# Decays of the first batch as TensorE products in the score banks of a fused attention and MoE kernel

## The chip, the cores and the metric

The kernel runs on one core of one Trainium2 chip. The metric is the device time of one launch in microseconds (us), the median of several runs; for the kernel before it is 889.91 us over three runs (888.77 to 890.62). Differences below about 0.2% (1.8 us) cannot be told from no change. The names of the engines are those of the profile: PE is TensorE (PEld its weight loads), ACT is ScalarE, DVE is VectorE, POOL is GpSimd, SP is SyncE, which issues the DMAs.

## The reference

Eight batches of eight heads, 576 positions, head size 64. Each head's scores get a decay (the difference of two cumulative sums of log f) and a causal mask, then a softmax; the attention output, 4608 rows of 512, goes through three matrices whose products are maximised and a fourth one.

```
scores = scale * np.matmul(q, k.transpose(0, 1, 3, 2))          # B, H, S, S = 8, 8, 576, 576
cum    = np.cumsum(np.log(np.clip(f, 0.0001, 1.0)), axis=-1)
decay  = cum[:, :, :, None] - cum[:, :, None, :]
scores = np.where(causal, -1e9, scores + decay)
attn   = np.exp(scores - scores.max(-1, keepdims=True))
attn   = attn / (attn.sum(-1, keepdims=True) + 1e-9)
x      = (attn @ v) laid out as (4608, 512)
h      = max(x @ w1, x @ w2, x @ w3)                              # 512 -> 768
out    = h @ w_out                                               # 768 -> 512
```

A query's own cumulative sum is the same for all its keys and falls out of the softmax; only the key's, with a minus sign, has to be added to the scores.

## The kernel before

Scores are held with keys on partitions and queries on columns. Two methods are in use.

**First batch (8 heads, as 4 pairs).** q and k are loaded in natural order (`load_raw`) and turned by TensorE (`turn_pair`, L568), since this is ready soonest. `scores_pair` (its products are L867) computes a pair of heads at a time: head 0 of the pair uses the array's rows 0 to 63, head 1 rows 64 to 127, each with its own PSUM bank. The 576 queries are cut into four tiles (`TILES`): tile 0 has 256 queries, tiles 1 and 2 have 128, tile 3 has 64; a tile covers 2, 3, 4 and 5 key blocks of up to 128 keys, 14 blocks a pair and head, 1600 columns. For each tile and head:

- pass a (L867): q and k products in fp32 for each block, then the mask as a product of an identity with a mask tile (L874);
- the maximum over a query's keys: ACT copies the first block out of PSUM with the key's decay as its bias (L895); DVE takes the other blocks one by one, adding their decay and taking the maximum in one instruction (L901); POOL's `partition_all_reduce` then takes the maximum over the partitions (L904);
- pass b (L886): TensorE subtracts that maximum from the bank (a product with a matrix that holds -1 in row 0 of each half);
- the exponential, once for each block, again with the block's decay as bias (L911).

The decays for the biases come from the cumulative sum (`decay`): five transposes on TensorE (L530) and two copies by DVE put the negated sums of the first eight heads into `CT`, keys on partitions. For the later batches the negated sums, split into a high and a low part, go to DRAM (`cdram`) and come back as two extra rows of k. `values_first` (L931 products with v, L941 sums), `finish_first` (row sums to DRAM and back, the division) and `split_first` (high and low part of x) follow.

**Later batches (56 heads).** `scores` (products L747, maxima L806 and L813, POOL L816, exponentials L830) takes a head at a time from loaded and transposed data; here decays are already in the products.

**The MoE part** (`moe`, `gemm1` L1092, `gemm2` L1123) runs in fp32r with high and low parts, three products for one. Its weights (12 loads of 1 MB) arrive as raw words, are converted on ACT and DVE (`convert`, L584, L587, L589) and split (`split`, L594, L595). All of TensorE's gemm work of a batch is interleaved with the scores of the next.

**What sets the order.** The kernel does not issue instructions in the order in which it is written. Every step is handed to a planner (`Plan.add`) with an engine, a cost, what it reads and writes, and a due time (`prio`); `Plan.emit` runs a list schedule over these costs and issues the steps in the order that comes out, a fixed order for each engine. `MOVES` is a table of 41 shifts of due times, most of them drawn from a seed. `GATES` names the steps after which the first six weight loads may be issued. `Slot` objects let a step take any free PSUM bank; `retire` orders the reuse of buffers under another name. Within an engine instructions start in that order only, so one that waits holds up all behind it.

```
add("ACT", act_cost(blocks[0][2]), lambda j=j, m=m: nc.scalar.activation(
    m, bank(j)[:, 0:nq], AF.Identity, bias=bias(0, j)), [kb[j], "ct"], [ks[j]], prio)
...
add("ACT", act_cost(w), lambda j=j, c=c, w=w, col=col, to=to, p=p: nc.scalar.activation(
    p[0:nk(c), to:to + w], bank(j)[0:nk(c), col:col + w], AF.Exp, bias=bias(c, j)), [kb[j], "ct", "ct4"],
    [f"e{pi % 2}/{t}{j}{c}"], prio, drop=(slots[j],))
```

Of the kernel before, what the change touches and what calls it, by code (L numbers as in the profile page):

```python
# [277 lines left out]
def kernel(  # L278
# [69 lines left out]
    LX = sb("pl2", [P, P + S1])  # L348
    LESS = LX[:, 0:P].bitcast(F32R)
    HLT = sb("hl", [P, 2, 2, 2, S], F32R)  # L350
    HL = {"k": HLT[:, 0], "q": HLT[:, 1]}
    CSX = sb("pl1", [P, 2 * S])
    CS = CSX[0:BH].bitcast(F32R).rearrange("p (t s) -> p t s", t=2)
# [10 lines left out]
    CT = sb("ct", [P, 5 * H])  # L364
# [149 lines left out]
    def decay():  # L514
# [1003 lines left out]
```

## Time and profile before

| | |
|---|---|
| median of three runs | 889.91 us (888.77 to 890.62) |
| profiled execution, device time | 891.11 us |
| its span, first to last instruction | 889.3 us |
| outside the span | 1.81 us |
| PE busy in the span | 865.4 us (97%) |
| DVE, ACT, POOL busy | 651.5, 406.4, 360.1 us |
| mean granted TensorE clock | 0.987 of 2.4 GHz |
| weights and other DMA traffic | 111.48 MB |

Busy time counts a stretch once, however many instructions of the engine overlap in it; a group's busy time in a list by lines adds the instructions up. A busy PE is not a PE at its peak: at the lower granted clock it does half the work in the same time. The granted clock has two levels, 1.2 and 2.4 GHz, so that a mean of 0.89 over a stretch says that 22% of it ran at 1.2 GHz. The wait of an instruction is put down to the engine whose work ended last before it started.

### The profile page before, as it was taken

Reading aid. Unit: us, or ns where it says so; the run is one execution under the profiler, and the core shown is the slowest. Engines: PE = TensorE matmul, PEld = TensorE weight load, DVE = VectorE, ACT = ScalarE, POOL = GpSimd, SP = SyncE. Lnnn points to the kernel's source line nnn. Section 1 sums busy time; section 2 is a strip of 40 time slices with the busy share of each in tenths; the row PEclk is TensorE's granted clock in tenths of the full one; section 3 lists DMA queues with packets and bytes.
Section 4 is the critical chain, followed back from the end, with each engine's and each line's share of the span. In section 5 each row is a group of like instructions: output and inputs, shape, how many; then the busy total and the mean of one; then the engine's idle time right before and its main releaser. Section 6 shows DMA issues by size and latency. Waiting matters only on the chain.

```text
span 889.3 us, 17657 instructions
## 1 busy us (share of the span) xinstructions
PE 865.4 (97%) x6437; PEld 772.7 (87%) x6437; DVE 651.5 (73%) x1405; ACT 406.4 (46%) x1014; POOL 360.1 (40%) x200
## 2 busy tenths in 40 slices
PE   8977899999999999999999999999999999999998
PEld 5655788898988999998988989898998989899997
DVE  3566896758767786678777786578867697788990
ACT  4787663545434443445334453344434443344431
POOL 2342322144455355544554355535544544540000
PEclk9888899999999999999999999999999999999999
DMA  7637867654555454564455355455545464300001
GB/s 168 200 99 196 268 165 178 162 134 138 114 149 143 102 144 102 146 145 122 120 142 141 92 152 126 134 120 158 120 103 155 104 169 97 92 11 15 24 1 60
DMA packets 99518, 111.48 MB, mean 125 GB/s; under 512 B 61432, under 2 KB 62200, under 8 KB 99432
## 3 DMA queue, kind: packets, MB, share of 16 engines
q1 hardware_dynamic: 99432, 110.35, 47.2%
q8 instruction: 51, 0.84, 0.4%
q14 instruction: 35, 0.29, 0.1%
HBM read 50.74 MB, written 9.88 MB: 68 GB/s over the span
## 4 chain that ended last, share of the span: by engine, by line
PE 93%; ACT 4%; DMA 1%; SPq 1%; DVE 1%; POOL 1%; issue 0%; ACTq 0%; DVEq 0%; POOLq 0%
PE s L1092 25%; PE mp L1092 15%; PE s L1123 10%; PE mp L1123 6%; PE t L1092 6%; PE s L747 5%; PE mp L747 4%; PE mp L1005 4%; PE s L1005 3%; PE s L1288 3%; PE mp L1288 2%; PE t L1005 2%; PE t L747 1%; PE t L1288 1%; ACT w L911 1%; PE s L931 1%
## 5 line engine op out<-in xcount | busy, mean ns | idle before, releaser
L845 POOL PARTITION_ALL_REDUCE z<-va_s x48 | 174.5, 3635 | 272.7 <-DVE va_s L840 134.2
L1092 PE MATMUL s<-xh_r,w_r 128*128 128x256 f32 (+1 forms) x1096 | 259.5, 297 | 0.0
L1092 PEld LDWEIGHTS s<-xh_r,w_r 128*128 128x128 f32 x1096 | 189.1, 188 | 4.0 <-issue 2.2
L1092 PE MATMUL mp<-xh_r,w_r 128*128 128x256 f32 (+1 forms) x672 | 165.5, 296 | 0.0
L816 POOL PARTITION_ALL_REDUCE gm<-mx x56 | 118.0, 2108 | 114.7 <-DVE mx L806 92.5
L1092 PE MATMUL s<-xl_r,w_r 128*128 128x256 f32 (+1 forms) x548 | 161.8, 295 | 0.0
L1092 PEld LDWEIGHTS mp<-xh_r,w_r 128*128 128x128 f32 x672 | 118.4, 188 | 2.8 <-issue 2.2
L1092 PEld LDWEIGHTS s<-xl_r,w_r 128*128 128x128 f32 x548 | 103.0, 188 | 0.9
L1092 PE MATMUL mp<-xl_r,w_r 128*128 128x256 f32 (+1 forms) x336 | 99.1, 295 | 0.0
L647 DVE STREAM_TRANSPOSE hl<-hl 128x576 f32<-128x576 f32 x56 | 66.2, 1240 | 16.7 <-DMA hl<-in_k_dram 7.3
L747 PE MATMUL s<-qs_r,ks_r 128*128 128x320 f32 (+4 forms) x334 | 71.9, 297 | 1.8 <-POOL qs_r L818 1.8
L1123 PE MATMUL s<-w_r,hmh_r 128*128 128x512 f32 x216 | 68.8, 400 | 0.0
L1092 PE MATMUL t<-xh_r,w_r 128*128 128x320 f32 (+1 forms) x248 | 67.7, 305 | 0.0
L747 PE MATMUL mp<-qs_r,ks_r 128*128 128x320 f32 (+4 forms) x256 | 60.3, 298 | 4.0 <-DMA ks_r<-hl 4.0
L1092 PEld LDWEIGHTS mp<-xl_r,w_r 128*128 128x128 f32 x336 | 63.1, 188 | 0.3
L1106 ACT ACTIVATE hmh_r<-tm 128x256 fp32r<-128x256 f32 x84 | 34.9, 416 | 60.7 <-DVE tm L1103 60.2
L1108 DVE TENSOR_TENSOR hml_r<-tm,hmh_r 128x256 fp32r<-128x256 f32 x84 | 53.5, 638 | 7.7 <-ACT hmh_r L1106 7.3
L747 PEld LDWEIGHTS s<-qs_r,ks_r 128*128 128x128 f32 (+1 forms) x334 | 53.3, 182 | 5.7 <-POOL qs_r L818 2.5
L1103 DVE TENSOR_TENSOR tm<-s,tm 128x256 f32<-128x256 f32 (+1 forms) x88 | 39.4, 449 | 21.2 <-ACT tm L1101 9.6
L806 DVE TENSOR_TENSOR mx<-mx,s 128x320 f32<-128x320 f32 (+3 forms) x112 | 47.3, 422 | 6.6 <-ACT mx L813 3.2
L747 PEld LDWEIGHTS mp<-qs_r,ks_r 128*128 128x128 f32 (+1 forms) x256 | 42.2, 181 | 7.3 <-DMA ks_r<-hl 4.4
L1092 PEld LDWEIGHTS t<-xh_r,w_r 128*128 128x128 f32 x248 | 46.2, 192 | 1.3 <-issue 1.0
(461 smaller groups left out, 1978.1 us busy)
## 6 DMA issues: line engine op xcount, KB each, us to landing
qs_r<-hl SPq DMA_DIRECT2D x168, 144.0 KB
ks_r<-hl SPq DMA_DIRECT2D x168, 144.0 KB
w<-in_moe_w_dram SPq DMA_DIRECT2D x9, 1024.0 KB
out_dram<-o_r SPq DMA_DIRECT2D x35, 256.0 KB
hl<-in_k_dram SPq DMA_DIRECT2D x14, 576.0 KB
hl<-in_q_dram SPq DMA_DIRECT2D x14, 576.0 KB
r_r<-rdram SPq DMA_DIRECT2D x56, 144.0 KB
vn<-in_v_dram SPq DMA_DIRECT2D x30, 128.0 KB
```

Source lines behind the costliest of these rows:

```text
L647: add("DVE", 1085, lambda e=e, tt=tt, xs=xs: nc.vector.transpose(tt[:, e], xs[:, e]), [key + "0"], [key + "1"], prio)
L747: nc.tensor.matmul(bank[bk][0:l.shape[-1], col:col + w], l, rhs(qa, w), start=start and bk not in begun, stop=stop, skip_group_check=True)
L806: nc.vector.tensor_tensor(mt[:, a:a + w], mt[:, a:a + w], bank[bk][:, col:col + w], op=ALU.max)
L816: add("POOL", 450 + 2.6 * nq, lambda: nc.gpsimd.partition_all_reduce(gm, mt, P, bass.bass_isa.ReduceOp.max), [km, km + "a"], [kg], prio - ...
L845: add("POOL", 520 + 5.1 * nq, lambda: nc.gpsimd.partition_all_reduce(Z[:, 0:S], blocks_sum()[:, 0:S], P, bass.bass_isa.ReduceOp.add), ["s1 ...
L1005: nc.tensor.matmul(t[D * j:D * j + D, qa:qa + w], vn[:, j, c, 0:D], prs[u][j][0]()[:, col:col + w], start=y == 0, stop=True, skip_group_ch ...
L1092: nc.tensor.matmul(m(), unit_w(i, fb)[:, w, kt, :], xx, start=kt == 0 and x == 0, stop=kt == KT - 1 and x == 2,)
L1103: add("DVE", dve_cost(cn), lambda m=m: nc.vector.tensor_tensor(t, m(), t, op=ALU.max), [km, kt_], [kt_], prio + EV, drop=(slot,))
L1106: add("ACT", act_cost(w) + 40, lambda hh=hh, a=a, d=d, w=w: nc.scalar.activation(hh()[:, fb, d:d + w], t[:, a:a + w], AF.Copy), [kt_], [kh ...
L1108: add("DVE", dve_cost(w), lambda hh=hh, hl=hl, a=a, d=d, w=w: nc.vector.tensor_tensor(hl()[:, fb, d:d + w], t[:, a:a + w], hh()[:, fb, d:d ...
L1123: nc.tensor.matmul(BANKS[slot.bank][:, 0:cn], l[:, fb, cs], unit_o(fb)[:, r, ds], start=fb == 0 and x == 0, stop=fb == FT - 1 and x == 2,)
L1288: nc.tensor.matmul(bank[c](), w(tw)[:, k], mat(x)[:, tx, k], start=new and k == 0 and z == 0, stop=k == 1 and z == 2, skip_group_check=True)
```

## The change

For the first batch the key's decay no longer comes in as a bias of ACT and DVE instructions, but is added to the score bank by TensorE.

- `decay()` no longer turns the sums for `CT`. DVE writes their negated high part to partitions 0 to 31 of a tile `BT` and the low part to 32 to 63; ACT copies both to partitions 64 to 127. `SEL` is a selection matrix with a one where a partition's head is the wanted one, made from the identity.
- `scores_pair` gets a step `decays()` between pass a and the maxima: one fp32r product for each block and head, whose stationary operand is the block's part of `BT` (64 rows) and whose moving operand is one column of `SEL`, broadcast over the block's queries. That makes 28 products a pair, 112 in all.
- Maxima: one `tensor_reduce` over all of a tile's blocks for each head, read from PSUM, 32 in all in place of 80 instructions of DVE. Only tile 0, whose blocks have different widths, keeps a copy on ACT (of 128 columns, 8 in place of 32).
- Exponentials: no bias, so one instruction takes several blocks: 384 columns in tiles 0, 1 and 2, a further 128 in tile 2, and 192 and 128 in tile 3. 48 in all in place of 112.
- The sums for the later batches (`CS`) lie in `MX` and `GM` and go to DRAM in two DMAs; row sums and reciprocals of the first batch lie elsewhere; mask products of tile 3 have 128 output rows.
- The planner's table `MOVES` has 783 entries in place of 41, and due times (`A2`, `B1`, `WP`), `GATES`, and some planner costs differ. This moves instructions in the whole program.

```
-    CT = sb("ct", [P, 5 * H])
+    CS = MX[0:BH].bitcast(F32R), GM[0:BH]
...
+    CSX = sb("pl1", [P, 2 * S], F32R)
+    BT, LESS, SEL = CSX[:, 0:S], CSX[:, S + 256:S + 384], CSX[:, S + 384:S + 384 + H]
...
-        add("PE", 400, turn, ["pf1", "idf"], ["sp2"], DP, rows=H)
-        add("DVE", 130, lambda: nc.vector.tensor_scalar(CT[:, 0:4 * H], SP2[:, 0:4 * H], -1.0, None, op0=ALU.mult), ["sp2"], ["ct"], DP)
-        add("DVE", 110, lambda: nc.vector.tensor_scalar(CT[0:64, 4 * H:], SP2[0:64, 4 * H:5 * H], -1.0, None, op0=ALU.mult), ["sp2"], ["ct4"], DP)
...
+        x = PF[1][0:32, 0:S]
+        add("DVE", 369, lambda: nc.vector.tensor_scalar(BT[0:32], x, -1.0, None, op0=ALU.mult), ["pf1"], ["bt0"], DP, port=1.0)
+        add("ACT", act_cost(S), lambda: nc.scalar.activation(BT[64:96], BT[0:32].bitcast(F32), AF.Copy), ["bt0"], ["bt2"], DP)
+        add("DVE", 669, lambda: nc.vector.scalar_tensor_tensor(
+            BT[32:64], x, -1.0, BT[0:32].bitcast(F32), op0=ALU.mult, op1=ALU.subtract), ["pf1", "bt0"], ["bt1"], DP, port=1.0)
+        add("ACT", act_cost(S), lambda: nc.scalar.activation(BT[96:128], BT[32:64].bitcast(F32), AF.Copy), ["bt1"], ["bt3"], DP)
...
+        def decays():
+            for c, qa, w, col in blocks:
+                for j in range(2):
+                    one = SEL[half(j), 2 * pi + j:2 * pi + j + 1].broadcast_to((D, w))
+                    nc.tensor.matmul(bank(j)[0:nk(c), col:col + w], BT[half(j), keys(c)], one, start=False, stop=False,
+                                     skip_group_check=True)
...
         for j in range(2):
             m = mt[:, nq * j:nq * j + nq]
-            add("ACT", act_cost(blocks[0][2]), lambda j=j, m=m: nc.scalar.activation(
-                m, bank(j)[:, 0:nq], AF.Identity, bias=bias(0, j)), [kb[j], "ct"], [ks[j]], prio)
-
-            def most(j=j, m=m):
-                for c, qa, w, col in blocks[1:]:
-                    x = m[0:nk(c), qa - q0:qa - q0 + w]
-                    nc.vector.scalar_tensor_tensor(x, bank(j)[0:nk(c), col:col + w], bias(c, j), x, op0=ALU.add, op1=ALU.max)
...
+            if t == 0:
+                add("ACT", act_cost(P), lambda j=j, m=m: nc.scalar.activation(m[:, 0:P], bank(j)[:, 0:P], AF.Copy),
+                    [kb[j]], [ks[j] + "a"], prio - CB)
+                m, src, c = m[:, P:], lambda j=j: bank(j)[:, P:384], 2
+            else:
+                src, c = lambda j=j: bank(j)[:, 0:n], len(blocks)
+            add("DVE", 1.05 * n + 150, lambda j=j, m=m, src=src, c=c: nc.vector.tensor_reduce(
+                m, src().rearrange("p (c q) -> p q c", c=c), axis=AX.X, op=ALU.max), [kb[j]], [ks[j]], prio - CB)
...
+                runs = [(0, 3 * nq, lambda p=p: p[1][:, 0:3 * S1].rearrange("p (c y) -> p c y", y=S1)[:, :, q0 - S2:q0 - S2 + nq], x)]
+                if t > 1:
+                    runs.append((3 * nq, n, lambda p=p: p[1][:, 960 + P * (t == 3):960 + P * (t == 3) + n - 3 * nq], lambda v: v))
+            for y, (a, e, dst, view) in enumerate(runs):
+                add("ACT", act_cost(e - a), lambda j=j, a=a, e=e, dst=dst, view=view: nc.scalar.activation(
+                    dst(), view(bank(j)[:, a:e]), AF.Exp), [kb[j]], [f"e{pi % 2}/{t}{j}{y}"], prio, drop=(slots[j],))
...
-        (11.3, 13.3, 0, 21, 0.03), (-20, 100, 1, 61, -0.8), (1.4, 5.4, 0, 4533, 1), (25.8, 26.3, 0, 29917, 0.06),
+        (2.1, 10.1, 0, 43247, 1), (33.3, 34.3, 0, 27900, 0.12), (-20, 100, 1, 22, -0.8), (-5.9, 2.1, 0, 23458, 0.5),
...
-    LEAD, MLAG, WP, WR = 2.1, 2.0, 2.7, 0.65
+    LEAD, MLAG, WP, WR = 2.1, 2.0, 1.0, 0.65
-    A2, A1, B1, UB, TO, XO1 = 0.8, 1.6, 0.4, 0.1, (1, 3, 2), 0.6
-    GATES = ("vn1/0", "vn3/0", "e1/200", "vd0/1", "vd1/1", "vd2/1")
+    A2, A1, B1, UB, TO, XO1 = 0.3, 1.6, 1.5, 0.1, (1, 3, 2), 0.6
+    GATES = ('vn1/0', 'vn3/0', 'e1/000', 'e1/100', 'vd1/2', 'vd1/1')
```

Three places show what moves. On PE, tile 0 of the first pair; L874 are the masks of the kernel before, followed there by warm-up products (L547):

```order
L874 LDWEIGHTS ident
L874 MATMUL s_110<-mask,ident 128x128
L874 LDWEIGHTS ident
L874 MATMUL mp_115<-mask,ident 128x128
L874 LDWEIGHTS ident
L874 MATMUL s_110<-mask,ident 128x128
L874 LDWEIGHTS ident
L874 MATMUL mp_115<-mask,ident 128x128
L547 LDWEIGHTS ident
L547 MATMUL s_108<-ident 128x512
```

The same tile in the changed kernel; L1085 are the masks, L1091 the decays (`pl_70` is the tile that holds `BT` and `SEL`):

```order
L1085 LDWEIGHTS ident
L1085 MATMUL mp_113<-mask,ident 128x128
L1085 LDWEIGHTS ident
L1085 MATMUL t<-mask,ident 128x128
L1085 LDWEIGHTS ident
L1085 MATMUL mp_113<-mask,ident 128x128
L1085 LDWEIGHTS ident
L1085 MATMUL t<-mask,ident 128x128
L1091 MATMUL mp_113<-pl_70 128x256
L1091 MATMUL t<-pl_70 128x256
L1091 MATMUL mp_113<-pl_70 128x128
L1091 MATMUL t<-pl_70 128x128
```

Four products of 64 array rows now stand behind the four masks of 128 rows, two for each head.

On ACT, the exponentials of tile 3 of the first pair before the change (`pf` and `ph` are the two heads):

```order
L911 ACTIVATE pf_76<-t,ct 128x64
L911 ACTIVATE ph_78<-s_109,ct 128x64
L911 ACTIVATE pf_76<-t,ct 128x64
L911 ACTIVATE ph_78<-s_109,ct 128x64
L911 ACTIVATE ph_78<-s_109,ct 64x64
L911 ACTIVATE pf_76<-t,ct 128x64
L911 ACTIVATE pf_76<-t,ct 64x64
L911 ACTIVATE ph_78<-s_109,ct 128x64 x2
L911 ACTIVATE pf_76<-t,ct 128x64
```

And the same tile after it (L1135; L793 before and the tile-0 exponential behind are its neighbours):

```order
L793 ACTIVATE ks_68<-mp_114 128x96x3
L1135 ACTIVATE pf_76<-s_109 128x3x64
L1135 ACTIVATE pf_76<-s_109 128x128
L1135 ACTIVATE ph_78<-s_110 128x128
L1135 ACTIVATE ph_78<-s_110 128x3x64
L1135 ACTIVATE pf_77<-mp_112 128x384
```

Ten instructions have become four, and `ct` is no longer read.

On PE again, the last rows ahead of the first gemm product (L1092) in the kernel before; L747 are scores of the second batch:

```order
L747 MATMUL t<-qs_r,ks_r 128x192
L747 MATMUL s_109<-qs_r,ks_r 64x64
L747 MATMUL mp_114<-qs_r,ks_r 128x448
L747 MATMUL s_110<-qs_r,ks_r 128x256
L747 MATMUL s_111<-qs_r,ks_r 128x448
L747 MATMUL s_108<-qs_r,ks_r 128x256
L760 LDWEIGHTS ident
L760 MATMUL s_111<-mask,ident 128x128
L760 LDWEIGHTS ident
L760 MATMUL s_108<-mask,ident 128x128
L1092 MATMUL t<-xh_r,w_r 128x256
```

In the changed kernel the first gemm product (L1315) stands right behind the row sums of the fourth pair (L1164):

```order
L1164 MATMUL s_108<-w_97,rx_r 32x160 x2
L1164 MATMUL s_108<-w_98,rx_r 32x160 x2
L1164 MATMUL s_108<-w_97,rx_r 32x160 x2
L1164 MATMUL s_108<-w_98,rx_r 32x160
L1164 MATMUL s_108<-w_97,rx_r 32x160
L1315 MATMUL s_107<-xh_r,w_r 128x256
L1315 MATMUL s_107<-xl_r,w_r 128x256
```

Ahead of the first gemm product there are 18 score products of the second batch before the change (three passes of six) and 6 after it (one pass); the other two passes have moved behind it.

## Rows read from the trace of the kernel before

**Rows 1.** Windows of the core: busy us (x instructions) of each engine, clock, DMA
```profile
core 0: us, PE busy (x) PEld busy (x) DVE busy (x) ACT busy (x) POOL busy (x), PEclk, DMA share, GB/s
0.00:96.20 96.20, 77.03 (x710) 52.87 (x710) 57.85 (x138) 64.69 (x198) 34.55 (x42) 0.89 0.65 177
96.20:120.00 23.80, 22.74 (x214) 20.55 (x213) 21.23 (x35) 19.63 (x36) 6.58 (x4) 0.95 0.83 235
120.00:870.00 750.00, 749.48 (x5430) 685.51 (x5430) 572.44 (x1233) 319.52 (x776) 318.95 (x154) 1.00 0.45 117
```

**Rows 2.** PE's waits to 96.2 us: who waited for whom, us, times, longest
```profile
PE mp L747 <- DMA ks_r<-hl: 3.6, 1, 3.6
PE mp L867 <- ACT w L911: 3.1, 1, 3.1
...
PE s L747 <- POOL qs_r L818: 1.8, 1, 1.8
PE s L547 <- POOL ident masks.py:199: 1.5, 1, 1.5
...
PE mp L568 <- DMA w<-in_k_dram: 0.6, 1, 0.6
...
PE mp L867 <- ACT ph L911: 0.3, 1, 0.3
```

**Rows 3.** The same windows view in steps of 5 us
```profile
20.00:25.00 5.00, 3.04 (x21) 2.13 (x21) 1.16 (x3) 5.00 (x21) 3.29 (x3) 0.85 0.74 144
25.00:30.00 5.00, 4.73 (x34) 4.02 (x35) 1.67 (x5) 3.34 (x11) 1.16 (x2) 0.50 1.01 390
...
60.00:65.00 5.00, 3.30 (x40) 2.36 (x33) 0.36 (x1) 4.63 (x20) 1.98 (x2) 0.94 0.17 35
65.00:70.00 5.00, 5.00 (x44) 3.58 (x44) 4.15 (x16) 3.12 (x11) 1.07 (x1) 0.50 0.93 294
```

**Rows 4.** Windows of line L911 alone (ACT exponentials with bias)
```profile
0.00:96.20 96.20, 29.30 (x112) 0.89 0.65 177
```

**Rows 5.** Windows of line L895 alone (ACT copies with bias)
```profile
0.00:96.20 96.20, 11.10 (x32) 0.89 0.65 177
```

**Rows 6.** ACT groups by shape to 130 us: x count, busy us, mean ns
```profile
L830 ACT ACTIVATE pf<-s 128x384 f32<-128x384 f32 x2 | 1.0, 502 | 0.0
...
L949 ACT ACTIVATE rx_r<-mp 128x128 f32<-128x128 f32 x3 | 0.8, 275 | 1.4 <-PE mp L941 1.4
```

**Rows 7.** Windows of line L901 alone (DVE maxima)
```profile
0.00:96.20 96.20, 24.48 (x80) 0.89 0.65 177
```

**Rows 8.** DVE groups by shape to 130 us (maxima of later heads, PSUM)
```profile
L806 DVE TENSOR_TENSOR mx<-mx,mp 128x448 f32<-128x448 f32 x1 | 0.6, 622 | 0.2 <-ACT mx L813 0.2
...
L806 DVE TENSOR_TENSOR mx<-mx,s 128x64 f32<-128x64 f32 x2 | 0.4, 220 | 0.2
```

**Rows 9.** Timeline of PE: start us, us, engine, line, instruction
```profile
48.97 0.29 PE L874 MATMUL s<-mask,ident 128*128 128x128 bf16 x2
49.19 0.18 PEld L886 LDWEIGHTS s<-gm,pl 64*128 64x128 f32 x1
...
61.24 0.27 PE L867 MATMUL mp<-qs 64*128 64x128 f32 x1
...
61.90 0.27 PE L867 MATMUL mp<-qs 64*128 64x128 f32 x1
```

**Rows 10.** Windows of line L530 alone (PE transposes of the sums)
```profile
0.00:96.20 96.20, 0.64 (x5) 0.55 (x5) 0.89 0.65 177
```

**Rows 11.** Windows of line L747 alone (PE scores of the second batch)
```profile
0.00:96.20 96.20, 4.40 (x18) 3.33 (x18) 0.89 0.65 177
96.20:130.00 33.80, 5.52 (x30) 4.24 (x30) 0.96 0.70 204
```

**Rows 12.** Timeline of SP: the DMA of the sums for later batches
```profile
11.17 0.56 SPq L472 DMA_DIRECT2D cdram<-pl  x1
```

More of the change, by code (lines that the diff above doesn't have):

```diff
@@ L549, in warm_up @@
         add("DVE", 165, lambda: nc.vector.tensor_copy(IDF, ident), ["const"], ["idf"], -6)
+        x = LX[:, 416:416 + H]
+        add("DVE", 150, lambda: nc.vector.tensor_reduce(
+            x, IDF.rearrange("p (g x) -> p x g", g=4)[:, 0:H], axis=AX.X, op=ALU.add), ["idf"], ["sel0"], -5)
+        add("DVE", 80, lambda: nc.vector.tensor_copy(SEL, x), ["sel0"], ["sel"], -5)
     def load_raw(pi, prio):
@@ L570, in go @@
                             start=x == 0, stop=True, is_transpose=True, skip_group_check=True)
-                add("PE", 340, go, [f"raw{pi}/{c}0", f"raw{pi}/{c}1", "idf"], [kp], prio, rows=96, take=(slot,))
+                add("PE", 400, go, [f"raw{pi}/{c}0", f"raw{pi}/{c}1", "idf"], [kp], prio, rows=56, take=(slot,))
                 to = dst.rearrange("d (p y x) -> d y p x", y=2, x=3)[:, y]
@@ L578, in turn_pair @@
                 else:
-                    add("ACT", act_cost(288) + 115, lambda to=to, ps=ps, sc=sc: nc.scalar.activation(
+                    add("ACT", act_cost(288) + 165, lambda to=to, ps=ps, sc=sc: nc.scalar.activation(
                         to, ps(), AF.Copy, scale=sc), [kp], [key], prio, drop=(slot,))
@@ L698 @@
     TILES = {
-        0: dict(q0=0, nq=256, blocks=[(0, 0, 256, 0), (1, 128, 128, 256)]),
-        1: dict(q0=256, nq=128, blocks=[(c, 256, 128, 128 * c) for c in range(3)]),
-        2: dict(q0=384, nq=128, blocks=[(c, 384, 128, 128 * c) for c in range(4)]),
-        3: dict(q0=512, nq=64, blocks=[(c, 512, 64, 64 * c) for c in range(5)]),
+        0: dict(q0=0, nq=256, blocks=[(0, 0, 256, 0), (1, 128, 128, 256)], parts=(0,)),
+        1: dict(q0=256, nq=128, blocks=[(c, 256, 128, 128 * c) for c in range(3)], parts=(0,)),
+        2: dict(q0=384, nq=128, blocks=[(c, 384, 128, 128 * c) for c in range(4)], parts=(0, 1)),
+        3: dict(q0=512, nq=64, blocks=[(c, 512, 64, 64 * c) for c in range(5)], parts=(0, 1)),
     }
@@ L891, in scores_pair @@
         add("PE", 4.04 * n / 2.4 + 65 * 2 * diag + 140, pass_a, [f"kq{pi}", "const"] + ([f"vd{pi - 2}/{1 + (t == 0)}"] if pi > 1 else []), kb, prio,
-            take=tuple(slots))
+            take=tuple(slots), rows=64 if t == 3 else 128)
+        add("PE", sum(max(0.4477 * x[2] + 3, 109) for x in blocks) + 60, decays, ["sel"] + [f"bt{x}" for x in range(4)], kb, prio,
+            rows=(98, 67, 67, 34)[t])
         for j in range(2):
             m = mt[:, nq * j:nq * j + nq]
-            add("ACT", act_cost(blocks[0][2]), lambda j=j, m=m: nc.scalar.activation(
-                m, bank(j)[:, 0:nq], AF.Identity, bias=bias(0, j)), [kb[j], "ct"], [ks[j]], prio)
@@ L898, in most @@
-            def most(j=j, m=m):
-                for c, qa, w, col in blocks[1:]:
-                    x = m[0:nk(c), qa - q0:qa - q0 + w]
-                    nc.vector.scalar_tensor_tensor(x, bank(j)[0:nk(c), col:col + w], bias(c, j), x, op0=ALU.add, op1=ALU.max)
-            add("DVE", sum(dve_cost(x[2]) + 128 for x in blocks[1:]) - 128, most, [kb[j], "ct", "ct4", ks[j]], [ks[j]], prio - CB)
+            if t == 0:
[4 more added lines that the diff above has]
+                src, c = lambda j=j: bank(j)[:, 0:n], len(blocks)
@@ L922, in values_first @@
         p = [PX[e][j][unit] for j in range(2)]
-        kp = [f"e{e}/{y}{j}{b[0]}" for y in TILES if (y == 0) == (unit == 2) for j in range(2) for b in TILES[y]["blocks"]]
+        kp = [f"e{e}/{y}{j}{b}" for y in TILES if (y == 0) == (unit == 2) for j in range(2) for b in TILES[y]["parts"]]
         nk = lambda c: slice(0, min(P, S - P * c))
@@ L1414, in exps @@
     def exps(e, j=None, unit=None):
-        return [f"e{e}/{t}{y}{b[0]}" for t in TILES if unit in (None, 1 + (t == 0)) for y in range(2) if j in (None, y) for b in TILES[t]["blocks"]]
+        return [f"e{e}/{t}{y}{b}" for t in TILES if unit in (None, 1 + (t == 0)) for y in range(2) if j in (None, y) for b in TILES[t]["parts"]]
     raws = [[f"raw{pi}/{c}{j}" for c in range(2) for j in range(2)] for pi in range(NP)]
@@ L1419 @@
     for i in range(2):
-        retire(raws[i], exps(1, i) + [f"z1/{i}"])
-    retire(["cs"], ["mp1/0", "mp1/1"] + [f"r1{e}/{j}" for e in range(2) for j in range(2)])
+        retire(raws[i], exps(1, i) + [f"r1{i}/{y}" for y in range(2)])
+    retire(["cs0"], [f"mp{t}/{j}" for t in (2, 3) for j in range(2)] + ["z1/1"])
+    retire(["cs1"], ["gp2", "gp3"])
     for pi in range(NP):
@@ L1436 @@
     for i in range(2):
-        retire(exps(1, i) + [f"z1/{i}"], [f"w{NW2 - 1 - i}"])
+        retire(exps(1, i) + [f"r1{i}/{y}" for y in range(2)], [f"w{NW2 - 1 - i}"])
         retire(raws[2 + i], [f"w{NW2 - 3 - i}"])
@@ L1459 @@
     moe(0, lambda x: H + lag + H * x)
[L1460 removed]
+    retire(["mp1/0", "mp1/1", "z1/0", "sel0"], ["pl2"])
     retire(["vn3"], ["s1", "s2"])
```

54 lines of the change are left out of this document (21 added, 33 removed), and 237 rows, old and new, of the table MOVES.

## Prediction

> **What bounds the kernel now.** I read the windows first, since averages over the whole span hide that this program has two regimes. From 120 to 870 us PE is busy 749.48 of 750 us at the full clock [rows 1]: nothing there can be gained by taking work from ACT or DVE, and PE's gemm work is the same after the change. What is left is the front, up to the first gemm product at 96.2 us. There PE is busy 77.0 us, idle 19.2, and the granted clock's mean is 0.89, so that 0.22 of the 96.2 us, 21 us, ran at 1.2 GHz [rows 1]. Next I read who PE waited for in the front. Nine entries name ACT's exponentials (L911), from 3.1 us down to 0.3, 11.4 us in all; the others of weight are 3.6 us for the load of a second-batch head, 1.8 for POOL's row of maxima of such a head, and 1.5 and 0.6 at the start, for the identity and the first load [rows 2]. So a wait on ACT ends last most often, though ACT is busy only 64.7 of the 96.2 us [rows 1]: the exponentials come in bursts behind each reduction, and PE has nothing else in its row. Last I read the clock in steps of 5 us: a step at 1.2 GHz follows one in which PE had gaps (3.04 busy of 5, then 0.50; 3.30 of 5, then 0.50) [rows 3]. Idle time is paid twice.
>
> **ACT.** The change takes 112 exponentials (29.3 us) and 32 copies (11.1 us) out of the front, 40.4 us [rows 4, 5]. It puts in 24 exponentials of 384 columns at 0.502, 16 of 128 and 8 copies of 128 at 0.275 each, and 8 of 192, by the slope between the two 0.33 [rows 6]: 12.0 + 4.4 + 2.2 + 2.6 = 21.2 us, and two copies of 576 columns, by the same slope some 0.67 each, 1.4 us. Sum 22.6, a saving of 17.8 us; ACT's front load falls to 46.9. These are durations without overlap, so 22.6 is the upper end; the kernel's own 112 exponentials overlap to 0.26 each, which would make it about 17.
>
> **DVE.** 80 instructions, 24.5 us [rows 7], become 32 reductions of 256 (tile 0), 384, 512 and 320 columns. The trace has no such reduction; the nearest rows are the maxima of later heads, also out of PSUM, 0.622 at 448 and 0.220 at 64 columns [rows 8], or 1.05 ns a column and 0.153. That gives 0.42 + 0.56 + 0.69 + 0.49 = 2.16 us a head and pair, 17.3 us for eight. Ends: 12.4 with no fixed part, 24.5 if a strided read costs what the block-wise maxima cost. I take 17.3. The two instructions for `BT` and the making of `SEL` add some 1.5. DVE's front load falls from 57.9 to 52: it is not the bound of the front either way, but see the second rival.
>
> **PE.** 112 products come in, in 56 concurrent pairs, since the two heads use different halves of the array (in a run of L867 at full clock, seven records of one head start from 61.24 to 61.90, each of 64 rows and 128 columns of weights, while the other head's run between them) [rows 9]. That is a pitch of 0.11, which I take for each of 14 blocks: 1.54 us for a pair of heads, 6.2 us in all. Ends: 2.7 if only the columns count (1600 a pair at 2.4 GHz), 15.1 if each pair takes the 0.27 us that a record lasts. Behind a mask the array changes from 128 rows to 64: two masks start at 48.97, the next products at 49.19, where two passes of 128 columns need 0.11 at full clock [rows 9]; the rest, 0.11, times 16 tiles is 1.8 us. The five transposes go, 0.64 us [rows 10]. Twelve of the 18 second-batch products move behind the front, 2.9 us of it [rows 11]; there they cost 2.2 at 0.184 each [rows 11]. The Trainium skill (TensorEngine Tiling (Array Packing), Tiling Modes) says that a change of tiling mode drains the engine; the 0.11 us agrees, and if it were paid on the way out of the decays too, the PE sum would be 1.8 higher.
>
> PE's front work, still at its present mix of clocks: 77.0 + 6.2 + 1.8 - 0.6 - 2.9 = 81.5 us. That is more than before; the gain has to come from waits and clock.
>
> **Waits.** The 11.4 us on ACT shrink with the ACT work that causes them, 22.6 for 40.4: to 6.4, 5.0 less. The load (3.6) and the row of maxima (1.8) concern products that have moved behind the front, so both go, except 1.0 that I leave for the one pass that stayed: 4.4 less. The start stays. Idle falls from 19.2 to 9.8, its half; as each stretch at 1.2 GHz follows gaps, I halve these 21 us as well, and 10.5 us more at 2.4 GHz give 5.3 back. The decays stand on PE between pass a and the maxima, so each tile's maximum comes 0.4 to 0.6 us later than its scores; behind it wait POOL's reduction and pass b, but other tiles' products stand between them in PE's row. For the first tile the high and low parts and their copies need three more instructions than `CT` did, about 1 us, hidden by the loads of k that it waits for anyway. What is late next is the fourth pair's row sums, and PE's own work.
>
> **Sum.** First gemm product at 81.5 - 5.3 + 9.8 = 86.0 us, 10.2 earlier; 2.2 come back behind it; the rest is as long as it is. So 8.0 us: the profiled execution would go from 891.1 (span 889.3) to 883.1, and the median, 1.2 below it, from 889.9 to **881.9**. Copies, DMAs for `CS` (one of 288 KB becomes two) and buffer moves I cost at nothing: they lie beside loads in the first 20 us, and were that cover gone, one more issue on SP would cost 0.6 us [rows 12].
>
> **Rivals.**
> 1. *The front becomes PE's own.* ACT's waits go altogether, only the 2.1 us at the start and the first load remain, and with no gaps the clock stays up: 81.5 - 10.5 + 2.1 = 73.1 us, 23.1 earlier, 20.9 net: 869.0. For it: ACT at 47 us of work has room in 73. Against: tiles still go through POOL, 34.6 us of it in one row [rows 1], with PE waiting between bursts.
> 2. *The gemm starts early and runs dry.* Its weights are converted on ACT and DVE; in 96 to 120 us DVE is busy 21.2 of 23.8 us [rows 1], so it is near its own bound there, and a gemm that starts 10 us sooner wants the same conversions 10 us sooner. If DVE gives back only the 5.8 us that it saved in the front, PE waits for the other 4.4: 886.3. For it: DVE's row. Against: DVE had 38 us idle in the front, and two of the weight gates now hang on earlier steps.
> 3. *Slower: POOL in ACT's place.* Each tile's pass b waits for a maximum that goes decays, DVE, POOL; POOL's 16 reductions run one after another, and the decays push each back. If PE's 19.2 idle us merely change their releaser, the clock stays as it is too: 81.5 + 19.2 = 100.7, 4.5 later, and 2.2 behind: 896.6. The change turns to a loss where idle and clock together give back less than 6.7 us, that is where idle falls by less than about 4 us. For it: PE's extra 7.4 us (6.2 + 1.8 - 0.6) come in any case, the waits' release is inferred from one execution. Against: in the front the waits that name ACT are six times the one that names a maximum of POOL [rows 2].
> That the reordered middle gains or loses something is no rival of size: there is half a microsecond of idle PE in 750.
>
> **Chances and range.** Forecast (876 to 886) 0.54; front at PE's bound (below 876) 0.18; run dry (886 to 890) 0.14; slower rival 0.14. A measurement here tells no change from one within 0.2%, 1.8 us. Below 888.1 lie the first two cases and most of the third: faster 0.81; within 0.2% the rest of the third and the edge of the slower one, 0.06; slower 0.13. The range runs from 871, near the first rival, to 889.5, leaving about 0.06 below and 0.13 above; it also holds the ends for the decays (2.7 to 15.1 us makes 878 to 891, little of it likely above 887) and for DVE, which counts only through the second rival.
>
> **What would show it.** Right: the first gemm product at 80 to 91 us; ACT's exponentials and copies at 17 to 23 us of busy time; decays at 5 to 9 us; PE's waits on the exponentials at about half; fewer than 15 us at 1.2 GHz; 120 us to the end unchanged. Wrong: a first gemm product after 93 us, or PE idle behind it with DVE's weight conversions as releaser, or waits that name POOL's or DVE's maxima for more than 8 us.

## The result, and where the time came from

The changed kernel takes 877.13 us (median of four, 875.23 to 879.40) against 890.26 for the kernel before (median of four): a ratio of 0.9856, 95% interval 0.9829 to 0.9884, so 13 us faster. The forecast was 881.9 within 871.0 to 889.5. Side and range are right. The sum behind them is not, and that its result came this near is in part luck, since two misses partly cancel: the front gains twice what was forecast, and more of it is lost behind.

The windows of the changed kernel, columns as in [rows 1], cut at its first gemm product (L1315), which starts at 75.9 us:

```profile
0.00:75.90 75.90, 69.94 (x800) 49.52 (x800) 46.77 (x85) 45.65 (x107) 33.36 (x40) 0.98 0.82 231
75.90:120.00 44.10, 42.05 (x372) 39.01 (x371) 41.16 (x68) 28.52 (x55) 13.34 (x8) 1.00 0.53 150
120.00:870.00 750.00, 746.98 (x5365) 681.08 (x5365) 551.52 (x1208) 312.71 (x765) 320.77 (x152) 1.00 0.45 116
```

Against [rows 1] the front is 20.3 us shorter: PE's idle time falls from 19.2 to 5.96 us and the mean clock rises from 0.89 to 0.98, so 3 us instead of 21 ran at 1.2 GHz. Behind the first gemm product the program is 5.7 us longer (798.8 us to the end of the span for 793.1): 2.3 us more busy, and 3.4 us more idle. The span falls by the difference, 14.6 us.

PE's waits in the front, as in [rows 2] (L1135 are the exponentials):

```profile
PE s L757 <- POOL ident masks.py:199: 1.5, 1, 1.5
PE mp L782 <- DMA w<-in_q_dram: 1.5, 2, 1.1
PE s L1154 <- ACT w L1135: 1.3, 3, 0.8
PE mp L1078 <- ACT w L1135: 0.5, 1, 0.5
PE t L1078 <- ACT ph L1135: 0.4, 1, 0.4
...
PE s L1103 <- POOL pl L1122: 0.2, 1, 0.2
PE s L1078 <- ACT w L1135: 0.2, 1, 0.2
```

The nine entries on the exponentials, 11.4 us in all, have become four with 2.4 us. The second-batch head's load and row of maxima are gone from the list, and POOL's maxima of the first batch, the slower rival, hold PE for 0.2 us. The 1.5 us for the identity, which was there before, is now the longest single wait.

### The profile page after: what moved, and what is told of

It reads as the page before. It is cut to its first block, busy times and chain, and to the rows that moved or that the text cites. A ratio compares the mean times of both kernels' runs of the same rounds, so it can differ in the third digit from the quotient of the medians.

```text
span 874.7 us, 17720 instructions
## 1 busy us (share of the span) xinstructions
PE 860.6 (98%) x6544; PEld 771.0 (88%) x6544; DVE 639.5 (73%) x1359; ACT 387.6 (44%) x928; POOL 367.5 (42%) x200
## 4 chain that ended last, share of the span: by engine, by line
PE 93%; DVE 2%; POOL 2%; ACT 1%; SPq 1%; issue 1%; DMA 0%; POOLq 0%; DVEq 0%; ACTq 0%
PE s L1315 20%; PE mp L1315 17%; PE s L1346 10%; PE t L1315 8%; PE s L961 5%; PE mp L1228 5%; PE s L1228 4%; PE mp L961 4%; PE t L1346 4%; PE mp L1346 3%; PE s L1511 3%; PE mp L1511 2%; PE s L1154 1%; PE s L1164 1%; PE mp L1078 1%; PE s L1078 1%
## 5 line engine op out<-in xcount | busy, mean ns | idle before, releaser
L1315 PE MATMUL s<-xh_r,w_r 128*128 128x320 f32 (+1 forms) x896 | 211.5, 301 | 1.4 <-DVE tm L1326 1.4
L1315 PE MATMUL mp<-xh_r,w_r 128*128 128x320 f32 (+1 forms) x760 | 181.1, 299 | 0.2 <-DVE tm L1326 0.2
L1315 PEld LDWEIGHTS s<-xh_r,w_r 128*128 128x128 f32 x896 | 154.3, 189 | 6.6 <-issue 5.5
L1315 PEld LDWEIGHTS mp<-xh_r,w_r 128*128 128x128 f32 x760 | 131.1, 188 | 3.7 <-issue 2.4
L1315 PE MATMUL s<-xl_r,w_r 128*128 128x256 f32 (+1 forms) x448 | 133.1, 297 | 0.0
L1315 PE MATMUL mp<-xl_r,w_r 128*128 128x320 f32 (+1 forms) x380 | 112.4, 296 | 0.0
L1315 PE MATMUL t<-xh_r,w_r 128*128 128x256 f32 (+1 forms) x360 | 88.2, 297 | 0.0
L1315 PEld LDWEIGHTS s<-xl_r,w_r 128*128 128x128 f32 x448 | 85.0, 190 | 0.6
L1315 PEld LDWEIGHTS mp<-xl_r,w_r 128*128 128x128 f32 x380 | 71.7, 189 | 0.6
L1315 PEld LDWEIGHTS t<-xh_r,w_r 128*128 128x128 f32 x360 | 63.2, 188 | 1.1 <-issue 0.7
L1020 DVE TENSOR_TENSOR mx<-mx,s 128x64 f32<-128x64 f32 (+3 forms) x128 | 54.1, 423 | 10.1 <-ACT mx L1027 6.7
L1315 PE MATMUL t<-xl_r,w_r 128*128 128x256 f32 (+1 forms) x180 | 52.9, 294 | 0.0
L1032 POOL CAST qs_r<-gm 1x576 fp32r<-1x576 f32 x56 | 46.7, 833 | 3.6
```

What stands on the lines that cost most here:

```text
L1020: nc.vector.tensor_tensor(mt[:, a:a + w], mt[:, a:a + w], bank[bk][:, col:col + w], op=ALU.max)
L1032: add("POOL", 130 + 0.9 * nq, lambda: nc.gpsimd.tensor_copy(QS(s)[96:97, 1, q0:q0 + nq], gm[96:97, :]), [kg], [kx], prio - CB, port=0.6 * ...
L1315: nc.tensor.matmul(m(), unit_w(i, fb)[:, w, kt, :], xx, start=kt == 0 and x == 0, stop=kt == KT - 1 and x == 2,)
```

## The experiments

Two theories stood behind "faster". The structure: lighter ACT and DVE let TensorE through. The order: the new table, due times and gates did it, whatever the instructions are. The edits below change what a step issues and leave the planner's steps and costs alone, so that each engine keeps its order, unless the order is the thing changed. (In the four runs in the old order that merge something, mask products of tile 3 also have 128 output rows, as in the change.) "First product" is the first gemm product of the profiled execution, one for each run. Each ratio is to executions of the kernel before that were measured beside that run; their medians lie between 888.6 and 890.3 us, so the ratios compare better than the medians.

| run | first product, us | median, us | ratio to before, 95% interval |
|---|---|---|---|
| before | 96.2 | 890.3 | 1 |
| changed | 75.9 | 877.1 | 0.9856 (0.9829 to 0.9884) |
| old order, exponentials merged | 86.7 | 881.2 | 0.9895 (0.9861 to 0.9928) |
| old order, exponentials without bias only | 87.0 | 880.5 | 0.9898 (0.9869 to 0.9928) |
| old order, maxima merged | 93.3 | 887.7 | 0.9979 (0.9952 to 1.0005) |
| old order, both merged | 88.0 | 883.4 | 0.9910 (0.9878 to 0.9942) |
| old order, both merged, products added | 88.2 | 888.4 | 0.9984 (0.9960 to 1.0008) |
| changed, old settings | 87.7 | 917.8 | 1.0292 (1.0239 to 1.0344) |
| changed, empty table | 78.5 | 904.8 | 1.0161 (1.0107 to 1.0215) |
| before, empty table | 92.3 | 911.6 | 1.0242 (1.0197 to 1.0286) |
| new order, exponentials by block | 78.1 | 877.8 | 0.9862 (0.9818 to 0.9906) |
| new order, maxima by block | 83.9 | 881.2 | 0.9899 (0.9862 to 0.9936) |
| new order, exponentials by block with bias | 92.6 | 888.7 | 0.9995 (0.9973 to 1.0017) |
| new order, all of ACT's and DVE's old work | 96.3 | 896.0 | 1.0080 (1.0051 to 1.0109) |

### Parts of the structure in the old order

Exponentials merged (the code here is shortened; tile 0 is shown):

```
-    p[0:nk(c), to:to + w], bank(j)[0:nk(c), col:col + w], AF.Exp, bias=bias(c, j))      # 112
+    p[:, 0:384], bank(j)[:, 0:384], AF.Exp)                                             # 48
```

> The kernel before with its own order, except that the first batch's exponentials are merged as in the change (48 for 112) and have no bias; the bias stays in the maxima, so the first batch's decays are left out of the exponentials alone. ACT loses some 14 us of the front, DVE and PE nothing. Theory (ACT's relief, by PE's idle time and the clock): first gemm product at 84 to 90 us instead of 96.2, time 878 to 884. Rival O (the new order did it): 0 to 2 us, time 888 to 890, first product after 94. Rival D (DVE's maxima were what held the chain): 887 to 890.

It gave 881.2 us and a first product at 86.7 us, as the theory had it. Maxima merged:

```
-    nc.scalar.activation(m, bank(j)[:, 0:nq], AF.Identity, bias=bias(0, j))
-    nc.vector.scalar_tensor_tensor(x, bank(j)[...], bias(c, j), x, op0=ALU.add, op1=ALU.max)
+    nc.vector.tensor_reduce(m[:, a:nq], bank(j)[:, a:n].rearrange("p (c q) -> p q c", c=c), axis=AX.X, op=ALU.max)
```

> The kernel before with its own order, except that the maxima are one reduction for each head and tile (32 for 80 DVE instructions, 8 ACT copies for 32), without the decays, which are left out of the maxima alone. DVE loses some 9 us of the front, ACT 9, PE nothing. Theory (ACT's relief by whatever part): 3 to 7 us, time 883 to 887. Rival D: 7 to 12 us, time 878 to 883, more than merged exponentials alone. Rival O: 0 to 2 us.

887.7 us: the theory's 883 to 887 is missed, and with an interval of 0.9952 to 1.0005 no gain is clear, though the first product of the profiled execution comes 3 us earlier. Both together:

> The kernel before with its own order, with merged exponentials and merged maxima together; the first batch's decays are left out and no decay products are put in. Theory: first gemm product at 76 to 84 us, time 870 to 877, PE idle in the front at most 9 us, under 8 us at 1.2 GHz. Rival O: first product after 92 us, time 885 to 890, since an order fitted to slow exponentials makes no use of fast ones.

This missed: the first product came at 88.0 us and the time was 883.4 us, no better than with the exponentials alone. The longest of PE's waits to the first product in the run with both:

```profile
PE mp L747 <- DMA ks_r<-hl: 5.1, 1, 5.1
PE mp L867 <- ACT w L917: 2.5, 2, 2.1
```

The waits on the exponentials have fallen to 4.7 us in four entries. But the score product of a second-batch head, which in the old order stands ahead of the gemm, waited 3.6 us for its load [rows 2], and now it waits 5.1 (5.2 with the exponentials alone merged). So a part of what ACT and DVE gave back has turned into a wait for a DMA. That the load as such then holds the old order is read from this list; no run moved it alone. The other part of the miss, in the execution profiled, is the clock, in a stretch that begins before the first merged maximum (at 16.35 us) and that the kernel before ran at 1.00:

```profile
10.00:15.00 5.00, 5.00 (x36) 3.79 (x34) 0.46 (x1) 0.95 (x3) 0.00 (x0) 0.50 0.98 210
15.00:20.00 5.00, 5.00 (x29) 3.18 (x28) 2.01 (x5) 0.45 (x2) 0.90 (x2) 0.50 0.87 190
```

Then nearly the whole structure, with products of the decays' shape behind the masks (the transposes for `CT` stay; the making of `BT` and the moved buffers are not in it):

```
+    for c, qa, w, col in blocks:
+        for j in range(2):
+            nc.tensor.matmul(bank(j)[0:nk(c), col:col + w], LESS[half(j), 0:nk(c)],
+                             LESS[half(j), 0:1].broadcast_to((D, w)), start=False, stop=False)
```

> The kernel before, its own order, with merged exponentials and maxima as in the run with both, and 28 more products of 64 rows a pair behind each tile's masks, in the place and shape of the decays; they add the same 1 to every score, so that the decays are left out. It is the whole structure of the change in the old order. Theory F (the structure gains little in the old order, where the second batch's loads and scores stay put): first gemm product at 90 to 95 us, 885 to 890 us. Rival S (the structure alone is the gain): 874 to 880 us.

888.4 us, which can't be told from no change: **the structure without its order shows no gain** (the interval allows one of up to 4 us). What the products cost can be read here by medians, 5.0 us (6.6 us by the two ratios), or by PE's work. The front windows of the two runs, without and with the products:

```profile
0.00:88.01 88.01, 73.82 (x709) 50.46 (x710) 49.05 (x90) 43.77 (x110) 37.25 (x42) 0.88 0.69 189
```

```profile
0.00:88.22 88.22, 76.12 (x822) 54.60 (x822) 49.49 (x90) 43.78 (x110) 34.14 (x42) 0.93 0.68 188
```

Less what the clock cost (0.12 of 88.0 and 0.07 of 88.2 us), PE's work is 63.3 and 69.9 us: 6.7 us for 112 products, an estimate good to about 1 us, since the clocks are rounded to 0.01. The forecast had 8.0: 6.2, and 1.8 for the change from 128 to 64 rows. In the changed kernel the decays (L1091) are busy for 8.85 us, overlaps with their neighbours included, within the prediction's 5 to 9, and its price for the change holds as well: the first decay starts 0.15 us after a mask, whose 128 columns take 0.05 at 2.4 GHz, so that 0.10 is left where it had 0.11.

```profile
52.18 0.22 PE L1085 MATMUL mp<-mask,ident 128*128 128x128 bf16 x1
52.33 0.32 PE L1091 MATMUL s<-pl 64*128 64x128 f32 x1
```

The executions of the second run lay between 882.2 and 891.3 us, and the profiled one (882.3) is among its fastest, so its trace does not show where its median loses the rest. The clock is not the reason: three executions at 890 us have a mean granted clock of 0.994, more than the profiled one's 0.992.

### What makes an exponential dear

The run with merged exponentials took two things out at once, instructions and their bias. So the bias alone went, in the old order:

```
-    AF.Exp, bias=bias(c, j))
+    AF.Exp)
```

> The kernel before, its own order, with the 112 exponentials of the first batch left as they are, block by block, but without their bias; the decays are left out of these exponentials. Theory B (the bias operand itself makes an exponential dearer): the 112 take 18 to 20 us of ACT's busy time instead of 29.3, most of what merging them gave, and the time is 881 to 885 us. Rival M (the number of instructions is what costs): 27 to 30 us of busy time, time 887 to 890.

The line of the exponentials in this run (112 of them; before, [rows 4]). In such a view of one line stand the stretch, its length, busy us (x instructions), and then clock, DMA share and GB/s of the stretch:

```profile
0.00:87.02 87.02, 19.34 (x112) 0.91 0.70 192
```

19.3 us for 29.3, and 880.5 us, which can't be told from the 881.2 with 48 merged ones. **The bias was the cost; the number of instructions moved no time that these runs can measure.** The same pair in the new order, exponentials by block without and with a bias (shortened; `ones` stands for a column of ones that the kernel already holds):

```
-    AF.Exp)                      # one for each run of blocks, 48
+    AF.Exp)                      # one for each block, 112
+    AF.Exp, bias=ones[0:nk(c)])  # the same with a bias
```

> The changed kernel, every engine's order kept, but each merged exponential is again one instruction for each block (112 in place of 48); ACT gets some 14 us more in the front, the rest is as it was. Theory (ACT's relief is the part of the structure that counts): first gemm product at 80 to 86 us instead of 75.9, 881 to 887 us. Rival D (DVE's reductions count): 0 to 2 us, 877 to 879.

> The changed kernel, its own order; only the exponentials are block by block and with a bias (a constant 1) as before, so that ACT alone gets its work back: 28 to 31 us of exponentials instead of 15.2. Theory A (ACT has room to spare in the new order, DVE has not): first gemm product at 77 to 81 us, 876 to 881 us, less than the 4 us that DVE's block-wise maxima cost. Rival (ACT's relief is the gain, as the prediction had it): first product at 82 us or later, 882 to 888 us.

By block without bias: 877.8 us, nothing lost. That missed the theory of its expectation, which had put 14 us of ACT's work on the number of instructions; it was 3.7 us (18.90 for 15.22, below), and the first product came at 78.1. With bias: 888.7 us, nearly the whole gain lost, with the first product at 92.6. That is the rival of that expectation, and the prediction's own view, not the theory. ACT in the run without bias, start, us, then what ran (x3: three back to back):

```profile
51.58 0.61 ACT L1139 ACTIVATE w<-s 128x128 f32<-128x128 f32 x3 [1.14 <-PE mp L1103]
52.07 0.64 ACT L1139 ACTIVATE w<-mp 128x128 f32<-128x128 f32 x3
```

and the same six in the run with bias:

```profile
53.15 0.88 ACT L1139 ACTIVATE w<-s,rx_r 128x128 f32<-128x128 f32 x3 [1.10 <-PE mp L1103]
53.92 0.89 ACT L1139 ACTIVATE w<-mp,rx_r 128x128 f32<-128x128 f32 x3
```

Three start 0.49 us after the first three, or 0.77 with bias: 0.09 us each. Over the front that is 28.75 us of exponentials for 18.90:

```profile
0.00:92.60 92.60, 28.75 (x112) 0.83 0.68 192
```

```profile
0.00:78.14 78.14, 18.90 (x112) 0.96 0.80 225
```

The Trainium skill (ScalarE: Activation LUTs, What ACT_TABLE_LOAD costs) says that each pointer operand adds about 93 ns to an activation; 28.75 less 18.90 over 112 is 88 ns, so the traces agree. The prediction did not use this.

How 13.5 us more on ACT than in the changed kernel (28.75 for 15.22) become 16.7 us of the front: the front window and PE's longest waits of the run with bias, and then steps of 5 us, both with columns as in [rows 1] and [rows 2].

```profile
0.00:92.60 92.60, 81.40 (x800) 55.50 (x800) 49.16 (x87) 58.92 (x171) 30.62 (x40) 0.83 0.68 192
```

```profile
PE s L1160 <- ACT w L1139: 4.4, 3, 1.8
...
PE s L1160 <- ACT ph L1139: 1.0, 1, 1.0
```

```profile
50.00:55.00 5.00, 4.55 (x47) 3.82 (x46) 2.19 (x5) 3.90 (x14) 2.04 (x2) 0.77 0.98 276
55.00:60.00 5.00, 3.47 (x22) 2.49 (x22) 3.44 (x8) 2.48 (x8) 3.79 (x5) 0.50 0.64 169
60.00:65.00 5.00, 4.76 (x23) 2.26 (x24) 3.92 (x8) 4.06 (x15) 1.86 (x1) 0.50 0.16 31
65.00:70.00 5.00, 5.00 (x51) 3.35 (x50) 0.00 (x0) 0.63 (x2) 0.00 (x0) 0.52 0.02 4
```

PE's idle time is 11.2 us, 5.2 more than in the changed kernel. The other 11.5 us are busy time with the same 800 products, and they are the clock's: 0.83 for 0.98, 31 us at 1.2 GHz for 3. From 50 us on PE has gaps, and then runs 15 us at about half the clock, though busy for 13.2 of them. The products that wait (L1160) are those with v. Each wait there is small, at most 1.8 us; the stretches at half the clock that follow cost more than the waits.

### DVE's part in the new order

```
-    nc.vector.tensor_reduce(m, src().rearrange("p (c q) -> p q c", c=c), axis=AX.X, op=ALU.max)
+    nc.vector.tensor_copy(m, src()[:, 0:w])
+    for y in range(1, c):
+        nc.vector.tensor_tensor(m, m, src()[:, w * y:w * y + w], op=ALU.max)
```

> The changed kernel, every engine's order kept, but the maxima are taken block by block again (112 DVE instructions in place of 32 reductions); DVE gets some 10 to 15 us more in the front. Theory (ACT): 1 to 4 us, first gemm product at 77 to 80 us, 878 to 881 us. Rival D: 6 to 12 us, 883 to 889 us.

The two lines of the maxima in this run, the copies and the maxima, and of the changed kernel, the reductions (L1120):

```profile
0.00:83.92 83.92, 8.52 (x32) 0.90 0.78 209
...
0.00:83.92 83.92, 20.84 (x80) 0.90 0.78 209
```

```profile
0.00:75.90 75.90, 15.67 (x32) 0.98 0.82 231
```

With 13.7 us more of DVE the first product comes 8.0 us later, the size that the rival named for the time, and the median 4 us, the edge of the theory's range; the two intervals still touch. Not all of the 8.0 us is DVE's: in the execution profiled the clock falls to 0.50 from 10 to 15 us (shown in the last section), before any block-wise maximum, and the first of them starts 2.5 us later than the first reduction of the changed kernel:

```profile
15.77 0.29 DVE L1122 COPY hmh<-t 128x128 f32<-128x128 f32 x1 [5.77 <-PE t L1091]
```

```profile
13.30 0.42 DVE L1120 TENSOR_REDUCE hmh<-t 128x128 f32<-128x256 f32 x1 [3.60 <-PE t L1091]
```

What DVE does to PE shows in two waits on POOL's maxima, 1.3 and 1.1 us, that the changed kernel does not have:

```profile
PE mp L1103 <- POOL gm L1127: 1.3, 1, 1.3
PE s L1103 <- POOL hml L1127: 1.1, 1, 1.1
```

The last run gives ACT and DVE all of their old work back (with a constant 1 as the bias) in the new order; ACT's copies stand there where DVE's step is planned:

> The changed kernel, its own order, with the decays on TensorE as they are, but ACT and DVE do the work of the kernel before: 32 copies and 112 exponentials with a bias (a constant 1, which changes nothing in a softmax), 80 block-wise maxima that add the same 1. Theory F (the order needs the lighter ACT and DVE): first gemm product at 84 to 92 us, 882 to 890 us. Rival O (the new order is the gain, the structure is not needed for it): first product before 79 us, 875 to 880 us.

896.0 us, slower than before, and slower than expected: **in the new order ACT's and DVE's old work costs more than the whole gain**. The run also carries the decays, which the kernel before did not have. Less their price (5.0 to 6.7 us above) it would come to 889 to 891 us, an estimate: the new order by itself then neither gains nor loses. The run that would show it, the new order with ACT's and DVE's old work and no decays, was not made.

### The order itself

```
-    MOVES = [ ... 783 entries ... ]   A2, B1, WP = 0.3, 1.5, 1.0   GATES = ('vn1/0', 'vn3/0', 'e1/000', ...)
+    MOVES = [ ... 41 entries ... ]    A2, B1, WP = 0.8, 0.4, 2.7   GATES = ("vn1/0", "vn3/0", "e1/200", ...)
```

> The changed kernel with the order settings of the kernel before: its table of 41 shifts, its due times and its weight gates. Theory (the structure gives the gain): first gemm product at 78 to 86 us, time 877 to 884. Rival O (the order gives it): first product after 92 us, time 887 to 895.

917.8 us: slower than both kernels by far, and outside the ranges of both theory and rival. Most shifts are drawn from a seed and a step's number, so the old table gives the steps of the new program other shifts than it gave the old ones; as a test of the old order on the new structure this run is unfair, and the run with the products above is the fair one. So both programs also ran with an empty table, each with its own due times and gates:

```
-    MOVES = [ ... ]
+    MOVES = []
```

> The changed kernel with its table of shifts empty, its due times and weight gates as they are. Theory F (the structure makes room in the front, but only an order fitted to it turns the room into time): 895 to 925 us, the first gemm product at 80 to 90 us as in the run with the old settings, and the loss behind it, as PE idle of 10 us or more. Rival S (the structure alone is worth the gain, the old settings were just bad ones): at most 885 us.

> The kernel before with its table of shifts empty, so that neither of the two programs has a fitted table. Theory F: 895 to 925 us; against the changed kernel with an empty table the structure is worth 0 to 15 us. Rival S: 890 to 900 us, and 10 us or more slower than the changed kernel with an empty table. Rival N (the structure is worth nothing without the new table): the same as, or faster than, the changed kernel with an empty table.

The windows of the changed kernel with an empty table, then of the kernel before with one:

```profile
0.00:78.50 78.50, 72.98 (x741) 52.50 (x741) 41.37 (x78) 40.48 (x100) 28.61 (x39) 0.85 0.65 180
78.50:120.00 41.50, 31.11 (x280) 26.11 (x281) 34.51 (x52) 24.19 (x45) 9.19 (x6) 0.84 0.68 196
```

```profile
0.00:92.33 92.33, 75.90 (x710) 49.96 (x710) 57.66 (x137) 62.85 (x198) 35.48 (x42) 0.89 0.65 184
92.33:120.00 27.67, 24.44 (x219) 21.75 (x220) 25.35 (x38) 20.11 (x38) 5.38 (x4) 0.94 0.80 242
```

Neither program has a fitted table. The changed program brings the first product 13.8 us forward but the time only 6.8. These differences are the structure's together with those of due times, gates and planner costs, which differ between the two runs. The gemm starts early and runs dry: from the first product to 120 us PE idles 10.4 us for 3.2. The longest wait behind the first product, in the run of the changed kernel with an empty table, is for POOL's row of maxima of a later head:

```profile
PE mp L735 <- POOL qs_r L806: 12.2, 4, 10.0
PE s L1089 <- DVE tm L1100: 3.7, 4, 1.8
```

Theory F's times hold in both runs, and the 6.8 us lie in its range of 0 to 15; only the first product, at 78.5 us, came before its 80 to 90. With the fitted order PE idles 2.05 us from the first product to 120 (window in the section on the result). Which part of the order matters, table, due times or gates, was not tried.

## Why the prediction was right in its size, and wrong in its steps

**The bound was right**: the front, PE waiting on ACT's exponentials. With ACT's old exponentials back, and nothing else changed, the gain is gone (888.7 us).

**ACT's saving was right in size and wrong in reason.** 48 exponentials take 15.2 us and 8 copies 2.0, so with the two copies for `BT` 18.6 us, in the bracket of 17 to 22.6. The line of the exponentials in the changed kernel:

```profile
0.00:75.90 75.90, 15.22 (x48) 0.98 0.82 231
```

But the prediction worked it out from how many instructions and how many columns, "24 exponentials of 384 columns". The runs show that three quarters of the exponentials' 14.1 us come from dropping the bias (29.3 to 18.9; 19.3 in the old order) and that merging (18.9 to 15.2) moves no time that can be measured.

**The front's sum**, step by step, against 77.0 + 4.5 of PE work, 5.3 back from the clock and 9.8 of idle:

| term | forecast, us | traces, us |
|---|---|---|
| PE's work, at an equal clock | +4.5 | +2.0 |
| back from the clock | 5.3 | 9.1 |
| idle PE | 9.8 | 6.0 |
| first gemm product | 86.0 | 75.9 |
| lost again behind it | 2.2 | 5.7 |
| span | -8.0 | -14.6 |

The clock's 9.1 is 0.11 of 96.2 less 0.02 of 75.9 us, an estimate, good to about 1 us by the rounding of the clock, and it counts the gaps inside the slow stretches too; the work is what is left of 77.03 and 69.94. Two steps of the prediction failed, each by 4 us. One is the waits on ACT, scaled with its work (below). The other is "I halve these 21 us as well": the stretches at 1.2 GHz fell by six sevenths, from 21 us to 3, in one stretch:

```profile
30.00:35.00 5.00, 4.36 (x62) 3.32 (x61) 4.71 (x6) 2.44 (x4) 4.51 (x4) 1.00 1.05 389
35.00:40.00 5.00, 4.46 (x34) 3.16 (x34) 4.89 (x8) 4.59 (x10) 1.07 (x1) 0.66 0.66 232
```

The first rival, the front at PE's own bound (73.1 us), had the front nearly right, in part by luck: it left 2.1 us of idle time where 6.0 remained, and had 2.5 us of work too much. The clock's loss went by whole stretches, not in proportion to the idle time. The first product, set at 80 to 91 us for a right forecast, came outside that, on the good side.

**The waits on ACT** were scaled with its work, to 6.4 us. They are 2.4 in the new order and 7.5 with the bias back, so they did not go in proportion to the work. In the old order they fell too, to 4.7 us in the run with both merged, but there the wait for the head's load grew from 3.6 to 5.1 us. The forecast that the wait for the load goes, since the product moves behind the front, held. What it did not say is that without the new order, of which that move is one part, the change shows no gain (888.4 us).

**"it is not the bound of the front either way"**, said of DVE, is not borne out: with 13.7 us more of it PE waits 2.4 us more for the maxima, and the median is 4 us longer, though the intervals touch. The profiled front's 8.0 us is too much for it, since 2.5 us of delay were there before DVE's first maximum.

**Behind the first product** the prediction had 2.2 us for the moved score products, and 2.3 us more busy time came. But it wrote "the rest is as long as it is", and the 3.4 us of idle time had no term. A little of the second rival's mechanism is there, but not its cause: PE waits 1.4 us for a maximum of the gemm by DVE, and no wait names the conversion of weights.

```profile
PE s L961 <- POOL qs_r L1032: 2.8, 1, 2.8
PE s L1315 <- DVE tm L1326: 1.4, 1, 1.4
PE t L961 <- POOL qs_r L1032: 0.6, 1, 0.6
```

The largest, 2.8 us up to 567.8 us, comes in the middle that the prediction had ruled out as "no rival of size". It belongs to this execution: none of the four runs with the changed kernel's order and other instructions has it in its list.

**The slower rival** was wrong here: with the decays between pass a and the maxima, POOL's reductions hold PE 0.2 us. Its arithmetic, that PE's added work makes the kernel slower where idle time and clock stay, was not put to the test as it stands. The run with ACT's and DVE's old work comes to 896.0 us, near that rival's 896.6, but by luck: there the clock fell to 0.82, while idle time fell too:

```profile
0.00:96.30 96.30, 83.20 (x799) 56.31 (x800) 57.15 (x134) 66.15 (x195) 36.96 (x40) 0.82 0.66 185
```

This window of its front has 13.1 us of idle PE, less than the 19.2 before.

## What to carry to other kernels

Price an instruction by its operands, not only by its columns: here a bias read from a tile cost a third of an exponential (0.09 of 0.26 us). Dropping it is what gained, while merging instructions gained nothing that could be measured; its price on TensorE, 5 to 7 us, ate the gain in the old order and not in the new one. Test a change in structure together with an order that fits it: in the old order this one showed no gain, and the new order with ACT's and DVE's old work was a loss. And a forecast for a stretch whose clock falls and rises should be made twice, with the gaps and without, since in these traces the clock's part came and went by whole stretches.

## What the runs showed of the hardware that was not expected

The bias: 0.09 us for each exponential, above. The clock: in the run with maxima by block it falls to 0.50 behind a step of 5 us in which PE was busy 3.31 us; in the run with a bias in the new order a step with 3.22 us busy, at the same place, is followed by 1.00. So the size of the gaps in a step alone did not tell.

```profile
5.00:10.00 5.00, 3.31 (x19) 1.56 (x18) 4.41 (x7) 3.40 (x6) 0.00 (x0) 0.96 1.19 191
10.00:15.00 5.00, 5.00 (x28) 3.70 (x28) 0.00 (x0) 2.18 (x5) 0.00 (x0) 0.50 1.11 199
```

```profile
5.00:10.00 5.00, 3.22 (x25) 1.96 (x24) 4.14 (x7) 3.55 (x7) 0.00 (x0) 1.00 1.11 204
10.00:15.00 5.00, 4.76 (x57) 3.67 (x54) 0.75 (x2) 1.94 (x6) 0.95 (x1) 1.00 0.93 190
```

And one of POOL's copies of a row of maxima, 0.66 us in the median of 56, took 4.05 us at 564 us in the changed kernel, and PE waited for it. The longest is 1.09 us in the kernel before and 2.24 us in the four runs that keep the changed kernel's order. The cause stays open.

```profile
561.62 2.04 POOL L1030 PARTITION_ALL_REDUCE gm<-mx  x1
563.73 4.05 POOL L1032 CAST qs_r<-gm 1x576 fp32r<-1x576 f32 x1
```
